# A fused linear-attention and feed-forward kernel on one core: the written order of its 1,487 steps, the engine of 188 of them and their ring places are replaced

## The chip, the cores and the metric

The kernel runs on one core of a Trainium2 chip. The metric is the device time of one execution in microseconds (us), taken as the median of several runs. A profile of one execution shows every instruction of the five engines: PE (TensorE, matrix products; its weight loads are shown as PEld), DVE (VectorE), ACT (ScalarE), POOL (GpSimd) and SP (SyncE, which issues most transfers). Times inside the profile count from its first instruction.

## The reference

Cosine-weighted linear attention over 8 batches, 8 heads, 576 tokens and 64 features per head, followed by a feed-forward layer. With `pos` the token number and `r = max(x, 0)`:

```python
def phi(x, c, s):
    r = np.maximum(x, 0.0)
    return np.concatenate([r * c, r * s], axis=-1)      # c, s = cos, sin of pi/2*pos/576
kv  = einsum('bhsf,bhsd->bhfd', phi(k), v)              # 128 x 64 per batch and head
z   = phi(k).sum(axis=2)
att = einsum('bhsf,bhfd->bhsd', phi(q), kv) / (einsum('bhsf,bhf->bhs', phi(q), z) + 1e-6)
x   = att as 4608 tokens x 512
out = leaky_relu(x @ w_in) @ w_out                      # w_in 512 x 2048, w_out 2048 x 512
```

All inputs and the output are float32 in DRAM; the kernel computes its products in float16 and sums in float32.

## The kernel before

**Tiling.** The 4,608 tokens are cut into nine groups of 512: group g below 8 holds the first 512 tokens of batch g, and group 8 the last 64 tokens of all eight batches. Each group passes the attention and then the feed-forward layer; the work of several groups overlaps.

**Attention of group g** (2 to 7 in the plain form). Loads of q, k and v (`lq`, `lk`, `lv`) go into staging slots. POOL clips q and k at zero in place (`rq`, `rk`, line 370). Eighteen half-steps `kc g.j` and `ks g.j` (j from 0 to 8; lines 376, 378 and 382, by engine ACT, POOL or DVE) multiply k by the cosine or the sine into the one tile `kp`; eight steps `q g.j.f` do the same for q. `v g.0` and `v g.1` cast v into the one tile `vm`. `kv g` is 72 small products on PE (line 440) over half of the array's rows; it needs all eighteen halves and both casts, and since `kp` and `vm` exist once, the halves of the next group cannot be written before it is through. `ko g` copies the sums out. Two transpositions by DMA, `qT g.0` and `qT g.1` (line 484), turn q; four steps `n g.j` (line 523, 8 or 16 products each) form numerator and denominator, `N g.j` divides on DVE (lines 534 to 539), and a third transposition by DMA, `xT g` (line 496), turns the result for the feed-forward layer.

**Feed-forward of group g.** Groups 0 and 1 form the first product plainly (`f`, line 603). From group 2 on both products use a seven-product scheme (Winograd's form of Strassen): sums `X g.n` of quarters of x, four units `f g.u.n` of seven products (line 742, four matmuls of 256 columns each), copies and sums of their banks (`b`, `s`, `u`, `y`, `z`, lines 388 and 656), the four activations `a`, `c`, `e`, `d` (line 766), sums `S g.n` of quarters of the activated values (line 656), products `F g.n.tt.h` (line 825, again four matmuls of 256 columns), partial sums `M g.n`, results `O g.n` and stores `D g.n`. The second product uses the scheme from group 1 on. Group 0 forms it plainly (line 626).

**Start.** `L...` load q, k, v of batches 0 and 1 and both weights; `cw` and `w` cast the weights to float16. 14 idle products, and ten more named `i.0` to `i.9` (line 307), stand on PE before there is work.

**The order.** The whole program is the string `ORDER` (line 31): every token is a step, and the loop at line 1060 emits the steps in that order. A letter behind a colon chooses the engine (`P` POOL, `A` ACT, `D` DVE); a number behind `@` chooses the ring place, that is the staging slot, output tile or PSUM place that the step's tile takes. Each engine works off its own instructions strictly in the order of the tokens; between engines semaphores hold a step until what it reads is written and what it overwrites is read. A token that stands early on one engine's list therefore says only what that engine does before and after it, not when.

```python
    engines = {"D": DVE, "A": ACT, "P": POOL}
    for token in ORDER.split():
        token, *places[:] = token.split("@")
        name, _, e = token.partition(":")
        f, args = steps.pop(name)
        f(*args, *([engines[e]] if e else []))
```

SP's list holds the loads, the stores and the 21 transpositions. A slot's next load has to wait until the last reader of the slot is through.

Of the kernel before, what the change touches and what calls it, by code (L numbers as in the profile page):

```python
# [13 lines left out]
P = 128  # L14
# [35 lines left out]
N1.0.0 F0.3.0 F0.3.2 F0.3.4 q2.3.0:P F0.3.6 kc1.6:A F0.3.8 v1.2:A lk2@0 F0.3.10 rk2 kc1.8:A  # L50
O0.2:A@1 kv1.1@0 F0.3.12 F0.3.14 ko1.1:A n1.0.1@1 N1.0.1 ks2.7:P O0.3:A@2 F0.0.14 O0.0:A@3
xt1.1.0@0 n1.1.1 N1.1.1 ks2.1:P q2.2.1:A q2.1.1:A q2.1.0:A F0.1.8 xt1.0.0@1 xt1.0.1@0 xo1.0.1:D
lv2.0@1 q2.3.1:A q2.0.0:A q2.2.0:A xo1.0.0:D kc2.2:A ks2.3:A F0.1.10 F0.1.12 xo1.1.0:D xt1.1.1@0
xo1.1.1:D kc2.3:A kc2.1:D F0.1.14 T3 kc2.6:P f1.0.0@1 f1.0.2 f1.1.0 kc2.7:A ks2.0:D f1.1.2
kc2.8:P e1.0 ks2.2:D ks2.6:A f1.10@0 f1.4.0 ks2.4:P ks2.5:A kc2.0:D f1.4.2 f1.5.0 kc2.4:D f1.5.2
# [24 lines left out]
F2.6.1.0 y3.1 kc5.0:P c3.1 n4.2 N4.2 f3.2.1 v5.0:P D2.2 f3.1.4 d3.1 lq6@3 f3.2.5 s3.2:A F2.6.1.1  # L80
q5.3.1:A n4.3 b3.2:D f3.2.6 ks5.3:P u3.2:A q5.3.0:P f3.3.1 f3.2.3 f3.2.2 kc5.2:A M2.6 N4.3 xT4
z3.2 e3.2 f3.2.7 b3.3:A y3.2 F2.5.1.1 ks5.6:A F2.7.0.0 q5.1.1:P F2.7.0.1 F2.7.1.0 F2.7.1.1
f3.3.6 ks5.2:A ks5.0:D M2.7 D1.5 a3.2 f3.3.2 f3.3.5 s3.3:D u3.3:A f3.3.7 O2.5@1 c3.2 S3.1b
f3.2.4 F2.4.0.0 q5.0.0:A d3.2 F2.4.0.1 y3.3 F2.3.0.0 lv6.0@2 ks5.4:A a3.3 F2.4.1.0 kc5.8:P
f4.0.1 F2.4.1.1 O2.4@2 f3.3.4 q5.1.0:A f3.3.3 z3.3 c3.3 X4.1:P X4.3:D F2.3.0.1 F2.3.1.0 F2.3.1.1
# [6 lines left out]
F3.5.0.0@1 D3.2 F3.7.0.0 kc6.7:P N5.2 F3.5.0.1 s4.1:A y4.1 f4.1.3 ks6.4:A rq7 z4.1 ks6.5:A d4.0
kc6.2:A ks6.2:P F3.5.1.0 kc6.4:P f4.2.5 f4.2.1 lk7@2 n5.3 F3.7.0.1 q6.3.0:A S3.4a F3.5.1.1
f4.1.4 N5.3 F3.7.1.0 F3.7.1.1 M3.7 e4.1 b4.2:A f4.2.6 s4.2:A xT5 f4.2.2 c4.1 S4.1a d4.1 S4.3a
O3.5@3 u4.2:A f4.2.3 z4.2 F3.4.0.0 F3.4.0.1 F3.4.1.0 a4.2 f4.2.7 y4.2 f4.3.1 F3.4.1.1 f4.3.5
F3.3.0.0 ks6.3:P e4.2 b4.3:A S4.2a f4.3.6 O3.4@0 D2.4 c4.2 u4.3:A S3.4b kc6.3:P X5.1:D S4.1b
f4.2.4 f4.3.2 ks6.8:A s4.3:A f4.3.7 y4.3 F3.3.0.1 F3.3.1.0 X5.2:D f4.3.3 kc6.8:P f4.3.4 kc6.1:P
# [999 lines left out]
```

## Time and profile before

| | |
|---|---|
| median of 3 runs | 276.03 us (275.15 to 276.07) |
| profiled execution: span from first to last instruction | 274.9 us |
| profiled execution: its own time | not given apart from the span; 1.1 us lie between the span and the median |
| TensorE's granted clock, mean | 0.995 |
| PE busy | 263.1 us, 96% of the span, 2,904 matmuls |
| DVE, ACT, POOL busy | 207.7, 187.5, 121.2 us |
| DMA | 57.59 MB moved, mean 209 GB/s |
| chain that ended last | PE 66%, DMA 17%, POOL 8%, DVE 4%, ACT 2% of the span |

The busy time of PE is an upper bound: the end of a matmul is modelled, and a pause shorter than the modelled tail of the matmul before it does not show. A row of a timeline gives its start, its length, the engine, the line, the operation with the tiles written and read, shapes, count, and in brackets how long the engine had been idle and what ended that.

### The profile page before, as it was taken

What the parts mean: (1) busy time and instruction counts of PE and PEld (TensorE: products, weight loads), DVE (VectorE), ACT (ScalarE), POOL (GpSimd) and SP (SyncE); (2) the same over time, 40 slices, a digit from 0 to 9 for tenths busy, and PEclk for the clock granted to TensorE, in tenths of its full rate; (3) what the DMA queues carried; (4) which work ended last, traced back from release to release, by engine and by line L of the source; (5) the groups of instructions that cost most, each with busy time, mean ns of one, the idle gap of its engine ahead of it and who ended that gap; (6) DMA issues with size and microseconds to landing.
All of it is one profiled execution on the core that took longest, in us unless ns stands there. A gap on an engine that the chain in (4) does not pass through costs nothing.

```text
span 274.9 us, 7175 instructions
## 1 busy us (share of the span) xinstructions
PE 263.1 (96%) x2904; PEld 221.6 (81%) x2904; DVE 207.7 (76%) x411; ACT 187.5 (68%) x332; POOL 121.2 (44%) x142
## 2 busy tenths in 40 slices
PE   8779999999999999999899999999999999999993
PEld 3466555555899898998799999999999899999982
DVE  4870589856989688958979978997788894588751
ACT  7845985897998879787596675675567546567300
POOL 2856223999167990975773758112114005000000
PEclk9999999999999999999999999999999999999998
DMA  7999999999999999999986693667281505020425
GB/s 235 369 393 383 399 408 374 341 198 346 185 246 295 272 205 337 290 237 281 263 297 149 102 211 113 136 129 188 70 176 55 117 17 138 1 79 0 155 55 135
DMA packets 77263, 57.59 MB, mean 209 GB/s; under 512 B 49456, under 2 KB 65840, under 8 KB 76848
## 3 DMA queue, kind: packets, MB, share of 16 engines
q1 hardware_dynamic: 76624, 56.63, 74.8%
q10 hardware_dynamic: 608, 0.52, 0.7%
q8 instruction: 22, 0.36, 0.5%
q14 instruction: 9, 0.07, 0.1%
HBM read 36.70 MB, written 9.44 MB: 168 GB/s over the span
## 4 chain that ended last, share of the span: by engine, by line
PE 66%; DMA 17%; POOL 8%; DVE 4%; ACT 2%; issue 1%; SPq 1%; POOLq 0%; DVEq 0%; ACTq 0%
PE ps L825 31%; PE ps_f L742 26%; DMA qst<-in_q_dram 5%; DMA w2st<-in_moe_w_out_dram 5%; POOL kp L378 3%; PE ps_h L603 3%; PE ps_num L523 3%; DMA w1st<-in_moe_w_in_dram 3%; DMA qpT<-qp 2%; DMA kst<-in_k_dram 2%; DVE ext L656 2%; PE ps_kv L440 2%; POOL kst L370 2%; PE ps_f L825 1%; POOL qst L370 1%
## 5 line engine op out<-in xcount | busy, mean ns | idle before, releaser
L825 PEld LDWEIGHTS <-g 128*128 128x128 f16 x640 | 62.0, 98 | 7.1 <-ACT g L612 0.2
L766 ACT ACTIVATE g<-ps_f 128x512 f16<-128x512 f32 x84 | 48.6, 597 | 22.5 <-PE ps_f L742 11.4
L825 PE MATMUL ps<-w,g 128*128 128x256 f16 x496 | 63.7, 273 | 0.0
L742 PEld LDWEIGHTS <-w 128*128 128x128 f16 x448 | 48.8, 114 | 0.9
L742 PE MATMUL ps_f<-xT,w 128*128 128x256 f16 x336 | 47.8, 273 | 0.0
L742 PEld LDWEIGHTS <-wext 128*128 128x128 f16 x336 | 36.5, 114 | 2.4 <-issue 1.6
L825 PE MATMUL ps<-T,ext 128*128 128x256 f16 x240 | 32.3, 273 | 1.1 <-DVE ext L656 1.1
L603 PE MATMUL ps_h<-xT,w 128*128 128x512 f16 (+1 forms) x144 | 29.3, 356 | 0.0
L825 PEld LDWEIGHTS <-ext 128*128 128x128 f16 x256 | 24.4, 98 | 4.0 <-DVE ext L656 1.4
L742 PE MATMUL ps_f<-X,wext 128*128 128x256 f16 x176 | 26.3, 273 | 0.9 <-ACT g L766 0.6
L656 DVE TENSOR_TENSOR ps_f<-ps_f,u 128x512 f32<-128x512 f32 x28 | 19.5, 695 | 7.3 <-PE ps_f L742 3.5
L388 ACT COPY u<-ps_f 128x512 f32<-128x512 f32 x24 | 14.1, 587 | 15.8 <-PE ps_f L742 15.8
L603 PEld LDWEIGHTS <-w 128*128 128x128 f16 x144 | 15.6, 114 | 10.1
L656 DVE TENSOR_TENSOR y<-ps_f,s 128x512 f32<-128x512 f32 x28 | 19.2, 686 | 4.5 <-PE ps_f L742 3.2
L766 ACT ACTIVATE g<-y 128x512 f16<-128x512 f32 x28 | 17.7, 632 | 4.2 <-DVE y L656 4.2
L656 DVE TENSOR_TENSOR osb<-ps,ext 128x512 f32<-128x512 f32 x23 | 15.8, 685 | 5.8 <-PE ps L825 5.0
L539 DVE TENSOR_TENSOR xs<-ps_num,rden 128x512 f16<-128x512 f32 x28 | 19.4, 692 | 1.0
L612 ACT ACTIVATE g<-ps_h 128x1024 f16<-128x1024 f32 x16 | 16.2, 1021 | 5.3 <-PE ps_h L603 5.3
L378 POOL TENSOR_SCALAR kp<-kst,cos_t 128x256 f16<-128x256 f32 x32 | 18.9, 598 | 0.2
L656 POOL TENSOR_TENSOR X<-xT,X 128x512 f16<-128x512 f16 x7 | 8.5, 1219 | 23.2 <-DVE X L656 14.3
L378 POOL TENSOR_SCALAR kp<-kst,sin_t 128x256 f16<-128x256 f32 x26 | 17.7, 683 | 1.8 <-ACT g L766 1.6
L742 PE MATMUL ps_f<-xT,wext 128*128 128x256 f16 x112 | 16.9, 273 | 0.0
(121 smaller groups left out, 478.1 us busy)
## 6 DMA issues: line engine op xcount, KB each, us to landing
out_dram<-osb SPq DMA_DIRECT2D x32, 256.0 KB, 4.1
qst<-in_q_dram SPq DMA_DIRECT2D x7, 1024.0 KB, 11.3
kst<-in_k_dram SPq DMA_DIRECT2D x6, 1152.0 KB, 7.6
vst<-in_v_dram SPq DMA_DIRECT2D x12, 576.0 KB, 6.7
w2st<-in_moe_w_out_dram SPq DMA_DIRECT2D x3, 1024.0 KB, 12.5
ext<-in_moe_w_in_dram SPq DMA_DIRECT2D x4, 512.0 KB, 9.2
vst<-in_v_dram SPq DMA_DIRECT2D x4, 288.0 KB, 6.8
kst<-in_k_dram SPq DMA_DIRECT2D x4, 288.0 KB, 6.2
```

What stands on the lines that cost most here:

```text
L370: POOL.tensor_scalar(out=t, in0=t, scalar1=FMAX, scalar2=0.0, op0=ALU.min, op1=ALU.max)
L378: eng.tensor_scalar(out=o, in0=i, scalar1=col, scalar2=1.0, op0=ALU.mult, op1=ALU.mult)
L388: nc.scalar.copy(o, i)
L440: nc.tensor.matmul(ps[:, o, (c - lo) * NE : (c - lo + 1) * NE], lhsT=st["kp", b][sl, c, j, :], rhs=vm[sl, c, j, :], start=(j == 0), stop=( ...
L523: nc.tensor.matmul(ps[lo:hi, h // 4, (h % 4) * NE : (h % 4 + 1) * NE], lhsT=qpT[:, h, lo:hi], rhs=kv[b][:, h, :],)
L539: nc.vector.tensor_tensor(out=xs, in0=ps[:, :, 0 : 4 * NE].rearrange("p a (b e) -> p a b e", e=NE)[:, :, :, 0:D], in1=rden.rearrange("p (a ...
L603: nc.tensor.matmul(ps[:, m % 2, lo:hi], lhsT=w1[m // 4, c][0][:, w1[m // 4, c][1], m % 4 : 512 : 4], rhs=xT[:, lo // P : hi // P, c, :], s ...
L612: nc.scalar.activation(g_tile(g)[:, 2 * i : 2 * i + 2, :], st["h", g, i], AF.Lrelu)
L656: eng.tensor_tensor(out=o, in0=a, in1=b, op=op)
L742: nc.tensor.matmul(ps[:, mi * HT : (mi + 1) * HT], lhsT=a[:, c, 2 * r0 + mi : 512 : 4], rhs=b[:, c], start=(n in (1, 5) and mi == 0 and c ...
L766: nc.scalar.activation(g_tile(g)[:, m : m + 2, r * HT : (r + 1) * HT], {"a": A, "c": y22, "e": E, "d": B_}[e].rearrange("p (m t) -> p m t" ...
L825: nc.tensor.matmul(ps[:, tt], lhsT=a[:, i, tt * P : (tt + 1) * P], rhs=b[:, i], start=(first and i == 0), stop=(i == NPR - 1 and (apart or ...
```

## The change

Only the string `ORDER` is replaced. The set of 1,487 steps is the same, and so are all functions. What differs is the order of the tokens, the engine letter of some steps and the ring places. In numbers of steps, before and after:

| steps | POOL | ACT | DVE |
|---|---|---|---|
| halves of k (`kc`, `ks`), groups 2 to 7 | 58, 77 | 36, 20 | 14, 11 |
| halves of q, groups 1 to 8 | 22, 32 | 30, 21 | 12, 11 |
| casts of v, groups 2 to 7 | 5, 7 | 4, 5 | 3, 0 |
| sums of x (`X`) | 11, 6 | | 17, 22 |
| sums of the first weight (`W`) | 2, 0 | | 6, 8 |
| casts of weights (`cw`, `w`) | 10, 4 | 2, 4 | 5, 9 |
| bank copies `b` | | 22, 27 | 6, 1 |

Between the same two attention steps SP's list now holds

```text
before: xT2 D0.1 lv3.1 qT3.0 qT3.1 D0.0 lk4 lv4.0 lv4.1 lq5 xT3
after:  xT2 qT3.0 lk4 D0.0 qT3.1 lq5 D0.1 lv4.0 lv4.1 xT3
```

and POOL's list, from the clipping of k of group 4 on,

```text
before: rk4 kc4.4 ks4.6 ks4.5 kc4.5 kc4.7 ks4.7 q4.1.1 v4.1 rq5 kc4.2 ks4.1 ks4.3 ks4.4 kc4.3 ks4.2 rk5
after:  rk4 kc4.4 kc4.3 ks4.3 q4.1.0 ks4.7 kc4.0 ks4.2 kc4.1 q4.1.1 q4.2.1 q4.3.1 ks4.0 ks4.8 rq5 v4.0 v4.1 q4.2.0 q4.3.0 q5.2.1 q5.3.0 q5.0.1 q5.2.0 rk5
```

The diff, cut to the lines that hold the steps spoken of:

```diff
--- before.py
+++ after.py
 ORDER = """
-Lq0.0@0 Lq0.1 q0.3.1.0:P q0.1.0.0:D Lv0.0@1 q0.1.1.0:P q0.3.0.0:D q0.0.0.1:A q0.3.0.1:A
...
-i.4@0 kv0.0@1 ko0.0:A n0.0.0@0 N0.0.0 kc0.7:A Lw1.3 cw.3:P n0.1.0 N0.1.0 kc0.0:A kv0.1@1 ko0.1:D
...
-e0.4 v1.1:D kp1.2.1 qt1.2@0 qo1.2:A F0.0.0@0 qt1.0@1 q1.1.0:D w1.2:A qo1.0:A w2.0:D w2.2:D
...
-f1.8@0 f1.9 e1.4 n2.3 N2.3 lq3@3 kc3.1:A ks3.2:A f1.14@1 f1.15 S1.1a lv3.0@0 D0.3 kc3.6:P S1.2a
...
-F1.1.0.0@1 F1.2.0.1 F1.1.0.1 lq4@1 F1.1.1.0 F1.1.1.1 M1.1:A F1.2.1.0 xT2 F1.2.1.1 F1.6.0.0@1
...
-f2.0.3 u2.0:A f2.1.1 f2.0.7 z2.0 q4.2.1:P y2.0 q4.3.1:P a2.0 f2.1.5 lk4@3 rk4 F1.5.1.0 kc4.4:P
...
-f2.3.4 X3.2:D a2.3 S2.3a F1.3.1.0 F1.3.1.1 O1.3@3 F2.1.0.0@1 d2.3 F2.1.0.1 v4.1:P kc4.1:A
...
-lk5@1 e3.0 ks4.4:P y3.0 b3.1:A kc4.3:P ks4.2:P kv4 F2.2.1.1 ko4:A rk5 ks5.5:P f3.1.6 f3.1.5
...
-q6.1.0:A kc5.6:P kv5 S3.2c S3.2a f4.1.1 v6.1:P e4.0 lk6@0 rk6 ks6.7:P f4.1.5 qT5.1 q6.2.0:P
...
-F5.2.1.0 X6.3:D F5.2.1.1 u6.0:A f6.0.7 q8.1.1:P S5.3b S5.4a kc7.8:D s6.0:A y6.0 ks7.3:A kv7
...
-F8.4.1.0 D8.5.0 O8.3.0@3 D8.3.0 D8.3.1 F8.4.1.1 O8.4@2 D8.4
...
+Lq0.0@1 Lq0.1 q0.1.0.0:P Lk0.0@0 Lk0.1 Lv0.0@3 q0.1.0.1:P q0.0.0.0:D q0.3.1.0:D q0.3.0.1:A
+q0.2.0.1:A q0.3.0.0:A q0.0.1.1:P q0.3.1.1:D v0.0:P q0.2.1.1:A q0.1.1.1:A q0.2.0.0:A q0.2.1.0:A
...
+Lw1.5 Lw1.7 Lw1.3 cw.2:P cw.1:P cw.5:P kv0.0@0 ko0.0:A qt0.2 kc0.0:D n0.0.0@0 i.1@1 qo0.2:D i.9@1
...
+f0.4.d f0.6.a@0 f0.7.a f0.6.d f0.7.d e0.3 f0.10@1 f0.11 e0.2 f0.12@0 e0.5 f0.13 F0.0.0@1 qt1.3@1
...
+f1.14@1 lv3.1 f1.15 F1.2.0.0@1 e1.4 F1.2.1.0 n2.3 kc3.3:A kc3.7:A e1.7 kc3.5:A q3.0.0:A ks3.3:A
...
+F1.7.1.0 F1.7.1.1 q3.3.0:A xT2 kc3.4:A X2.1:D f2.0.1 f2.0.5 X2.3:D W0.3:D X2.2:D kv3 b2.0:A s2.0:A
+f2.0.6 f2.0.2 f2.0.3 ko3:A W1.4:D S1.4b a2.0 qT3.0 u2.0:D q4.0.0:P X2.4:P lk4@1 rk4 kc4.4:P kc4.3:P
+ks4.3:P q4.0.1:A z2.0 f2.1.1 q4.1.0:P ks4.7:P kc4.0:P ks4.2:P f2.0.7 kc4.1:P e2.0 b2.1:A D0.0 qT3.1
+q4.1.1:P q4.2.1:P y2.0 f2.1.5 s2.1:A lq5@2 n3.0 F1.7.0.1 q4.3.1:P ks4.0:P ks4.8:P D0.1 S1.4a N3.0
+rq5 M1.7 f2.0.4 lv4.0@3 f2.1.2 f2.1.6 f2.1.3 lv4.1 d2.0 v4.0:P v4.1:P f2.2.1 n3.1 u2.1:A a2.1 c2.0
...
+F2.1.0.1 ks4.6:D ks4.4:D z2.3 kv4 lk5@1 rk5 ks5.5:P ks5.6:P kc5.1:P ks5.4:P kc5.0:P kc5.2:P kc5.4:P
+q5.3.1:P kc5.8:P ks5.1:P kc5.5:P ks5.3:P ks5.8:P ks5.2:P kc5.7:P ks5.7:P M2.1:A kc5.3:P e2.3 S2.1a
+F2.2.0.0 S2.3a X3.1:D X3.3:D X3.2:D F2.2.0.1 kc5.6:P ks5.0:P f3.0.1 b3.0:A F2.2.1.0 f3.0.5 s3.0:A
...
+y3.3 z3.3 f3.3.2 f3.3.4 xT4 c3.3 qT5.0 lk6@3 S3.1b X4.1:D F3.1.1.0 rq6 kv5 rk6 ks6.7:P a3.3 kc6.0:P
...
+f5.3.6 kv7 u5.3:A s5.3:A S4.4a O4.4@0 f5.3.7 c5.2 lq8.0@3 xT6 F5.1.0.0@1 f5.2.4 d5.2 y5.3 a5.3 S5.1b
...
+F8.7.0.0 F8.7.0.1 F8.2.0.1 F8.7.1.0 S8.4a F8.7.1.1 F8.5.1.0 O8.2:A@0 D8.2 M8.7 F8.5.1.1 F8.5.0.1
+O8.5.1@1 O8.5.0@3 S8.4b D8.5.1 F8.4.1.0 D8.5.0 F8.4.1.1 F8.4.0.0 F8.4.0.1 O8.4@2 D8.4 F8.3.1.0
+F8.3.1.1 O8.3.1@0 D8.3.1 F8.3.0.0 F8.3.0.1 O8.3.0@1 D8.3.0
```

More of the change, by code (lines that the diff above doesn't have):

```diff
@@ L50 @@
[L50 to L55, printed above, removed]
@@ L80 @@
[L80 to L85, printed above, removed]
@@ L92 @@
[L92 to L97, printed above, removed]
@@ new lines @@
+ks2.0:P ks2.4:P O0.3:A@3 n1.0.1@1 T2 lv2.1 lk3@1 N1.1.0 F0.0.12 N1.0.1 F0.0.14 n1.0.0@0 F0.1.6
+F0.1.8 n1.1.1 kc2.7:P O0.0:A@2 q2.1.0:A q2.0.0:A F0.1.10 N1.0.0 xt1.1.0@0 xt1.0.0@1 xt1.0.1@1
+F0.1.12 N1.1.1 xo1.0.1:D xo1.1.0:A q2.1.1:A F0.1.14 xt1.1.1@1 xo1.0.0:D f1.4.0 f1.0.0@0 xo1.1.1:A
+q2.3.1:A f1.0.2 f1.5.0 q2.2.0:D q2.2.1:A ks2.2:D kc2.2:A f1.5.2 f1.1.0 f1.1.2 f1.2.0@1 f1.4.2
+kc2.6:A ks2.3:D ks2.6:D e1.0 O0.1:D@1 ks2.1:A e1.2 kc2.0:A f1.2.2 f1.10@0 f1.11 rk3 kc2.1:D kc2.3:D
+kc2.8:D W0.4:D f1.3.0 f1.3.2 v2.1:A kv2 kc3.0:P T4 T3 qT2.0 lq3@3 kc3.1:P ks3.6:P rq3 q3.1.0:P e1.5
```

168 lines of the change are left out of this document (84 added, 84 removed).

## The prediction

> **What bounds the kernel now.** I read the head of the page first, then busy time by stretches, then the chain that ended last, and only then the timelines of the places that these point to. First two lines of the page, then the stretches (width, then busy time and count of PE, PEld, DVE, ACT, POOL, granted clock, share of the DMA engines, GB/s).
>
> ```profile
> span 274.9 us, 7175 instructions
> ...
> PE 263.1 (96%) x2904; PEld 221.6 (81%) x2904; DVE 207.7 (76%) x411; ACT 187.5 (68%) x332; POOL 121.2 (44%) x142
> ```
>
> ```profile
> 0.00:20.00 20.00, 15.18 (x187) 9.07 (x188) 14.12 (x39) 13.76 (x24) 11.12 (x21) 1.00 0.92 330
> 20.00:60.00 40.00, 39.82 (x388) 23.08 (x385) 25.62 (x47) 31.55 (x49) 21.15 (x19) 1.00 1.03 357
> 60.00:110.00 50.00, 49.27 (x590) 42.25 (x585) 39.77 (x85) 43.33 (x78) 32.18 (x33) 1.00 1.08 268
> 110.00:160.00 50.00, 48.66 (x595) 44.94 (x594) 42.95 (x77) 36.34 (x68) 34.35 (x41) 1.00 0.95 230
> 160.00:210.00 50.00, 50.00 (x567) 46.89 (x567) 41.12 (x85) 33.55 (x63) 17.91 (x26) 1.00 0.61 140
> 210.00:260.00 50.00, 49.96 (x505) 46.50 (x505) 38.78 (x74) 27.83 (x50) 4.47 (x5) 1.00 0.25 69
> 260.00:275.00 15.00, 10.19 (x94) 8.88 (x91) 5.38 (x10) 1.17 (x2) 0.00 (x0) 0.91 0.33 88
> ```
>
> PE sets the time from 20 us on: of its 11.8 us without work, 4.8 lie in the first 20 us, 4.8 in the last 15, and 2.3 between. But a pause shorter than the modelled tail of a matmul is not seen as idle, so I also count matmuls. Their pace comes from the chain of waits (start, length, engine, line, count):
>
> ```profile
> 157.43 0.87 PE ps L825 x8
> 158.31 1.25 PE ps_kv L440 x72
> ...
> 219.61 0.54 PE ps L825 x4
> ...
> 253.16 3.06 PE ps L825 x28
> ```
>
> A matmul of 256 columns takes 0.109 us (3.06 / 28), a step of four 0.44 (0.87 / 2), one `kv` 1.25; a step beside a change of array form takes 0.54, so a change costs about 0.10. An `n` step of eight I put at 0.26 (0.032 each, an estimate from 1.25 / 72 and 0.109). From 110 to 160 us, 595 matmuls hold two `kv` (144), six `n` (48) and 403 large ones: 2.5 + 1.6 + 43.9 = 48.0 of 50. So 2.0 us are lost there, of which 1.34 show as idle. The same count gives 1 to 2 us for 60 to 110, 1.1 for 160 to 210 and about nothing after. Past 60 us some 4 to 5 us are lost in all; 18 changes of form (five `kv` and four `n8`, in and out) take up to 1.8 of them. About 3.5 us is what a better order could win there.
>
> **What the change leaves alone.** The steps are the same, so PE has the same 2,904 matmuls. I counted the places where PE goes from the full array to half of it (`kv`, `n8`) or back: 28 in the old order and 28 in the new. At 0.10 each that is 2.8 us in both: 0. So the change can only move pauses.
>
> **The start.** 0, with bounds of -0.7 and +0.8. PE's pauses before 20 us wait for transfers and for the casts and divisions behind them:
>
> ```profile
> 12.42 0.75 PE L440 MATMUL ps_kv<-vm,kp 64*128 64x66 f16 x36
> ```
>
> ```profile
> 30.29 0.69 DVE L390 CAST w<-w2st 128x1024 f16<-128x1024 f32 x1 [1.63 <-DMA w2st<-in_moe_w_out_dram]
> ...
> 34.09 0.38 PE L626 MATMUL ps_o<-w,g 128*128 128x512 f16 x1
> ```
>
> The new order loads the same bytes in nearly the same sequence and reaches the first `kv` about as late: one 256 KB weight block now goes ahead of three parts of v, which by the 330 GB/s of the first stretch puts them some 0.8 us later, while DVE has less ahead of the first division. Whatever is won or lost is then cut off at the first product with the second weight. In the old order it stands behind 25.3 us of matmul work and ran at 34.09; the start has thus cost 8.8 us. In the new order `F0.0.0` stands behind 22.2 us (`f0.8`, `f0.9`, two transpositions and one `F0` step now follow it): 22.2 + 8.8 = 31.0. The cast of that weight ends at 30.29 + 0.69 = 30.98, and the transfer before it, unmoved in the queue, ends the wait. Three microseconds of cover are gone, and it just fits.
>
> **The inputs of `kv`.** POOL takes 19 more halves of k and ten more of q, and gives back sums and casts of weights. What this threatens is one chain: clip k when it lands, write eighteen halves, then `kv`; and the halves cannot start before the last `kv`. For group 4 the old order ran so (POOL, then SP):
>
> ```profile
> 88.51 2.11 POOL L370 TENSOR_SCALAR kst<-kst 128x2304 f32<-128x2304 f32 x1 [1.64 <-ACT u L388]
> 90.72 0.48 POOL L378 TENSOR_SCALAR kp<-kst,cos_t 128x256 f16<-128x256 f32 x1
> ...
> 93.87 0.69 POOL L378 TENSOR_SCALAR qp<-qst,sin_t 128x512 f16<-128x512 f32 x1
> 94.51 1.14 POOL L390 CAST vm<-vst 128x1152 f16<-128x1152 f32 x1
> 95.63 1.90 POOL L370 TENSOR_SCALAR qst<-qst 128x2048 f32<-128x2048 f32 x1
> ...
> 101.66 1.16 POOL L378 TENSOR_SCALAR kp<-kst,sin_t 128x256 f16<-128x256 f32 x1
> ```
>
> ```profile
> 68.48 3.41 SPq L496 DMA_TRANSPOSE xT<-xs  x1
> ...
> 73.64 6.54 SPq L484 DMA_TRANSPOSE qpT<-qp  x2
> ...
> 80.84 0.43 SPq L256 DMA_DIRECT2D kst<-in_k_dram  x1
> ```
>
> ```profile
> L378 POOL TENSOR_SCALAR kp<-kst,cos_t x32: 468/477/1425, 55.0 to 168.3; 128x256 f16<-128x256 f32 x32
> L378 POOL TENSOR_SCALAR kp<-kst,sin_t x26: 471/492/1690, 52.9 to 171.6; 128x256 f16<-128x256 f32 x26
> ...
> DMA to landing us min/median/max: 5.9/6.9/13.3
> ```
>
> ```profile
> 66.86 0.42 PE L523 MATMUL ps_num<-kv,qpT 128*128 128x66 f16 x8
> ```
>
> Now the new order, counted from the first matmul of `n2.3`. The transposition `xT2` follows 1.6 us later (66.86 to 68.48). SP then holds it for 3.4 us and the one `qT3.0` for 3.5, and issues `lk4` 6.9 after `xT2`, where the old order, with the second `qT` and two small transfers ahead, needed 12.4. So the lighter queue ahead of k is a gain of 5.5 us. Landing 6.9 (the median), clipping 2.1: 1.6 + 6.9 + 6.9 + 2.1 = 17.5. Then POOL has nine halves of k, four of q, the clipping of q5 and both casts of v: 9 x 0.48 + 4 x 0.69 + 1.90 + 2 x 1.14 = 11.3, in all 28.8. At the price that the halves had in the old stretch it is more: from 90.72 to 102.82, less 0.69, 1.14 and 1.90, twelve halves took 8.4 us, 0.70 each, and the sum is 30.8. PE comes to `kv4` after 58 steps of 0.44, five `n` and one `kv`: 27.9. It has 35.1 us for the same way in the old order. So PE waits 0.9 to 2.9 us, less up to 0.6 because the first half of `kv4` needs only the first cast of v. I take +0.5, with bounds of 0 and +2.4. I lean to the lower end because the new order puts DVE's sums with two operands in SBUF after `kv4`, and it was beside such sums that the halves took 0.70. If the cover is gone altogether, everything behind `kv4` moves by the wait. The same count for `kv5` and `kv7` leaves POOL about 2 us early at 0.48 and about 1 late at 0.70.
>
> **The small pauses past 60 us.** Two of the old ones (ACT and PE, then POOL, DVE and PE), and a sum of the same form that was not disturbed:
>
> ```profile
> 90.66 0.51 ACT L376 ACTIVATE kp<-kst,sin_t 128x256 f16<-128x256 f32 x1 [1.03 <-POOL kst L370]
> ...
> 91.71 0.60 PE L742 MATMUL ps_f<-X,wext 128*128 128x256 f16 x4 [0.56 <-ACT g L766]
> ```
>
> ```profile
> 71.37 0.75 DVE L656 TENSOR_TENSOR ext<-ext,g 128x512 f16<-128x512 f16 x2
> ...
> 132.53 2.12 POOL L370 TENSOR_SCALAR kst<-kst 128x2304 f32<-128x2304 f32 x1
> ...
> 132.67 2.25 DVE L656 TENSOR_TENSOR ext<-ext,g 128x512 f16<-128x512 f16 x1
> ...
> 134.98 0.61 PE L825 MATMUL ps<-T,ext 128*128 128x256 f16 x4 [1.13 <-DVE ext L656]
> ```
>
> At 90.66 ACT stood 1.03 us before a half of k that waited for POOL's clipping, and the activation behind it came late for PE. The new order leaves ACT 20 such halves instead of 36. At 132.67 a sum on DVE, of which two took 0.75 together at 71.37, ended only when POOL's clipping did. For the rest I counted, over both products of groups 2 to 8, how much PE work stands between a product and the product that needs its evacuation, less the evacuation itself: of 412 such links 27 have under 0.5 us to spare in the old order, 11 in the new; between `ko` and `n` the spare is 2 to 6.8 us in five of six groups, where it was 0.3 to 1.6. By that ratio, 3.5 x 16 / 27 = -2.1; since the two pauses above came from queues and not from short links, I take -1.7, with bounds of -3.5 and +0.5.
>
> The Trainium skill speaks against the change here: "SBUF — State Buffer", section "Who interferes with whom", says that VectorE and GpSimd share one pair of ports as an exclusive lock, and that a VectorE operation with two SBUF inputs fully blocks behind a GpSimd operation that reads SBUF. The rows at 132.53 and 132.67 agree: 2.25 us instead of about 0.4, ending 0.27 us after the other's end. By that rule more work on POOL means more such blocks, and this term would be positive; that is the third rival.
>
> **The end.** -0.7, with bounds of -0.9 and 0.
>
> ```profile
> 268.28 1.91 PE L825 MATMUL ps<-ext,g 128*128 128x256 f16 x16
> 268.54 0.42 DVE L656 TENSOR_TENSOR osb<-ps_f,ext 128x256 f32<-128x256 f32 x1 [0.51 <-PE ps_f L825]
> 270.23 0.69 DVE L656 TENSOR_TENSOR osb<-ps,ext 128x512 f32<-128x512 f32 x1 [1.26 <-PE ps L825]
> ```
>
> ```profile
> out_dram<-osb SPq DMA_DIRECT2D x2, 128.0 KB, 2.6
> ...
> out_dram<-osb SPq DMA_DIRECT2D x4, 64.0 KB, 2.0
> ```
>
> The old order ends with the 512-column result (0.69) and its 128 KB store (2.6); the new one with a 256-column result (0.42) and a 64 KB store (2.0): 0.27 + 0.6 = 0.9, less some queueing behind two larger stores.
>
> **The sum.** 0 + 0.5 - 1.7 - 0.7 = -1.9 on a span of 274.9: 273.0. The profiled execution's own time is not shown; its span lies 1.1 under the median of 276.03, and I carry these 1.1 over unchanged: 274.1.
>
> **The rivals.** First, **the pauses only change place**: as many queues meet as before, and 11 short links cost what 27 did. For it speaks that the two pauses quoted came from queues. Then only the end and `kv4` count: 276.0 - 0.7 + 0.2 = 275.5. That the change doesn't do what it says belongs here: the forms are as many as before, and no wait of PE in the chain is for SP.
>
> Second, slower: **POOL becomes the last input of `kv`**. Place: `kv4`, then `kv5` and `kv7`. Price: 2.4 + 1 + 1, less 0.7 at the end and 0.3 of small pauses: +3.4, 279.4. It decides from a mean of about 0.6 us per half of k on POOL. For it: 0.70 in the old stretch; POOL already 32 to 34 of 50 us busy between 60 and 160. Against: the median of 0.48.
>
> Third, **DVE held by POOL**: clippings fall on DVE's sums that PE waits for. Two more of the kind at 134.98, 2 x 1.13, with the small pauses otherwise unchanged: 276.0 + 2.3 - 0.7 = 277.6. Against: both orders have the same 16 clippings, and only one such wait of PE showed.
>
> **How the numbers follow.** Forecast 274.1: 0.48, its own range 271.8 to 275.4. First rival 0.25, second 0.17, third 0.10. What a measurement of this kernel can tell from no change is about 0.5%, 1.4 us, so faster means under 274.65. Three quarters of the forecast's chance lie there, and a quarter to a third of the first rival's: 0.36 + 0.07 = 0.43. The same: 0.12 + 0.15 + 0.01 + 0.05 = 0.33 of the four in turn. Slower: 0.24. The range for all: 271.0 to 278.5.
>
> **What would show it.** In the changed profile: 28 changes of form and the same pace of 0.109; the first second-weight product near 31; `kp` on POOL near 0.5 us in its mean, and no or under 1 us of wait before `kv4`; in the stretches from 60 to 260, less idle than 2.1 us and less than 4 us lost by count; the last store of 64 KB. A `kv` that waits for `kp` or `vm` on POOL by over 1.5 us, or DVE sums of over 2 us ahead of PE, makes me wrong, as does a first second-weight product later than 33.

## The result, and the profile after

**The new order is slower by about 0.6%.** Its median is 277.53 us (20 runs, 276.68 to 279.24) against 276.44 us for the old kernel beside it (20 runs); the ratio is 1.0060, 95% interval 1.0037 to 1.0083. This ratio, like those below, is worked out from the single runs, without those over 1.5% above the fastest of their kernel, and is not the quotient of the two medians (1.0039). The forecast was 274.1, faster. The profiled execution took 277.58 us with a span of 275.0. The first lines of its page (span; busy time of the engines):

```profile
span 275.0 us, 7178 instructions
...
PE 262.5 (95%) x2904; PEld 222.2 (81%) x2904; DVE 215.9 (79%) x411; ACT 177.3 (64%) x306; POOL 137.4 (50%) x168
```

The work has moved as the table of the change says: POOL has 16.2 us more, ACT 10.2 less, DVE 8.2 more. Where the time went shows in the stretches of the new kernel (columns as in the prediction: width, PE, PEld, DVE, ACT, POOL with counts, clock, DMA share, GB/s):

```profile
0.00:20.00 20.00, 16.23 (x193) 9.72 (x194) 13.16 (x34) 14.78 (x27) 12.68 (x23) 1.00 0.91 325
20.00:60.00 40.00, 35.43 (x298) 20.18 (x296) 28.61 (x50) 22.60 (x31) 31.94 (x26) 1.00 0.98 344
60.00:110.00 50.00, 49.72 (x630) 41.83 (x629) 45.84 (x83) 40.92 (x70) 33.02 (x39) 1.00 0.99 241
110.00:160.00 50.00, 50.00 (x624) 47.16 (x623) 42.25 (x83) 35.76 (x65) 35.77 (x50) 1.00 1.02 261
160.00:210.00 50.00, 50.00 (x588) 46.81 (x587) 42.27 (x83) 32.08 (x60) 22.88 (x31) 1.00 0.66 144
210.00:260.00 50.00, 49.98 (x482) 46.77 (x481) 37.37 (x72) 30.01 (x56) 1.16 (x1) 1.00 0.24 63
260.00:275.00 15.00, 11.17 (x103) 9.73 (x100) 6.40 (x12) 1.17 (x2) 0.00 (x0) 1.00 0.42 122
```

Only one stretch is worse, and it is the one in which the old order lost nothing: from 20 to 60 us PE is without work for 4.6 us (40 - 35.43), where it was 0.2. From 60 to 260 us it is 0.3 instead of 2.1, and the tail after the last matmul is shorter, too. Ahead of 20 us PE stands for 3.8 us instead of 4.8.

Four waits of PE make up 4.3 of these 4.6 us. PE's timeline (start, length, what it is, and in brackets the wait and what ended it):

```profile
31.39 0.59 PE L621 MATMUL ps_o<-w,g 128*128 128x512 f16 x2 [0.87 <-DVE w L385]
...
37.88 2.32 PE L621 MATMUL ps_o<-w,g 128*128 128x512 f16 x10 [0.70 <-DVE w L385]
...
45.48 0.74 PE L435 MATMUL ps_kv<-vm,kp 64*128 64x66 f16 x36 [1.32 <-POOL vm L385]
...
52.74 0.41 PE L553 MATMUL ps_numh<-kv,qpT 128*128 128x66 f16 x8 [1.43 <-DVE xs L534]
```

In order: `F0.0.0`, the first product with the second weight; `F0.3.4`, the first that needs that weight's second block; `kv1.0`, the first `kv` of group 1; and `n1.0.0`. The chain of waits of the new kernel from the landing of q of batch 1 on (start, length, what) says what lies behind the last two:

```profile
14.86 12.82 DMA qst<-in_q_dram
...
30.11 5.78 POOL qp L377 x3
...
37.27 2.93 POOL qp L377
40.20 4.61 POOL kp L377 x4
44.82 0.34 POOL vm L385
...
45.42 1.66 POOL kp L377
47.08 1.36 POOL vm L385
...
48.48 0.75 PE ps_kv L435 x36
```

POOL is never idle from 27.87 to 48.4 us: five halves of q, five of k and two casts of v, all of group 1, one behind the other, and PE's `kv1.0` waits for one of the casts. What lies behind `n1.0.0` is on DVE (its timeline, from the copy `O0.2` to the start of the division `N1.1.0`):

```profile
49.81 0.69 DVE L385 COPY osb<-ps_o 128x512 f32<-128x512 f32 x1 [1.90 <-PE ps_o L621]
50.42 1.24 DVE L651 TENSOR_TENSOR T<-w,T 128x2048 f16<-128x2048 f16 x1
51.58 0.15 DVE L529 TENSOR_SCALAR den<-ps_numh 128x8 f32<-128x8 f32 x1
```

DVE holds `O0.2` until PE has written the other bank of its tile, and behind it stand the weight sum `T2` and only then `N1.1.0`, whose result frees the place of `n1.0.0`.

Why POOL takes so long is in the groups by shape. First the old kernel up to 60 us, then the whole of the new one (busy us, mean ns of one):

```profile
L382 POOL TENSOR_SCALAR qp<-qst,cos_t 128x256 f16<-128x256 f32 x2 | 2.3, 1169 | 4.3 <-DMA qst<-in_q_dram 4.3
L378 POOL TENSOR_SCALAR qp<-qst,cos_t 128x512 f16<-128x512 f32 x1 | 0.7, 687 | 0.0
```

```profile
L373 POOL TENSOR_SCALAR kp<-kst,sin_t 128x256 f16<-128x256 f32 x41 | 23.8, 587 | 0.4
L373 POOL TENSOR_SCALAR kp<-kst,cos_t 128x256 f16<-128x256 f32 x36 | 18.3, 516 | 3.2 <-PE ps_kv L435 3.1
...
L377 POOL TENSOR_SCALAR qp<-qst,sin_t 128x512 f16<-128x512 f32 x3 | 8.0, 2683 | 0.0
L377 POOL TENSOR_SCALAR kp<-wext,cos_t 128x128 f16<-128x128 f32 x5 | 6.3, 1268 | 0.0
L377 POOL TENSOR_SCALAR qp<-qst,cos_t 128x512 f16<-128x512 f32 x2 | 4.3, 2171 | 9.5 <-DMA qst<-in_q_dram 9.5
```

There are two forms of a half on POOL. Groups 2 to 8 are clipped first (`rq`, `rk`) and then take two multiplications (line 378 before, 373 after): 0.69 us for 128x512. Batches 0 and 1 have no clipping step, so POOL takes the maximum with zero and the product in one instruction (382, 377), and that costs 1.17 us for half the size. Five halves of q of group 1, which DVE and ACT did before in 0.5 to 0.7 us each, take 12.3 us on POOL. The five halves of k of group 1, which ACT did before, and the two casts of v come on top, with 6.3 and 2.0 us.

**One count for all kernels.** PE's 2,904 matmuls at their undisturbed pace (0.109 us for 256 columns, 0.216 for 512) make about 253.8 us in every version (up to 2 us more with other prices for the small products, the same in every row), and the first starts at 1.2. What is left of a span is PE's loss up to the start of `kv2`, its loss from there to the last matmul, and the tail behind that: for the new kernel 1.2 + 253.8 + 12.8 + 3.4 + 3.8 = 275.0. Losses are from one execution each. Up to `kv2` the kernels with one and the same start agree within 0.6 us (8.5, 8.7 and 9.1 with the old one; 12.8, 12.6 and 12.8 with the new one); behind it the two profiles of the old kernel differ by 1.7.

| kernel | median us (runs) | ratio to old, 95% | loss to `kv2` | loss behind | tail |
|---|---|---|---|---|---|
| old, as shown before | 276.03 (3) | | 8.5 | 6.7 | 4.7 |
| old, second profile (`e8`) | 275.43 (1) | | 8.7 | 5.0 | 4.7 |
| new | 277.53 (20) | 1.0060 (1.0037 to 1.0083) | 12.8 | 3.4 | 3.8 |
| `e1` | 276.48 (12) | 1.0028 (1.0004 to 1.0052) | 10.6 | 4.9 | 4.0 |
| `e2` | 276.51 (12) | 1.0028 (0.9998 to 1.0058) | 12.7 | 3.9 | 3.9 |
| `e3` | 277.01 (12) | 1.0036 (1.0016 to 1.0057) | 13.5 | 3.2 | 4.0 |
| `e4` | 277.02 (12) | 1.0043 (1.0019 to 1.0066) | 11.5 | 4.2 | 3.9 |
| `e5` | **272.91** (12) | **0.9905 (0.9874 to 0.9936)** | 9.1 | 3.7 | 4.0 |
| `e6` | 278.88 (6) | 1.0120 (1.0081 to 1.0160) | 12.6 | 4.6 | 4.7 |
| `e7` | 276.61 (12) | 1.0036 (1.0006 to 1.0066) | 8.8 | 6.0 | 4.0 |
| `e9` | 276.14 (12) | 1.0019 (0.9993 to 1.0045) | 9.4 | 5.8 | 3.9 |
| `e10` | 277.19 (12) | 1.0045 (1.0022 to 1.0069) | 12.8 | 3.3 | 3.9 |

New against the old kernel's second profile: +4.1 to `kv2`, -1.6 behind, -0.8 at the end (unrounded), together +1.7, which is what the ratio makes of 276 us. The first profile was of a long execution: the median span of 35 executions of the old kernel is 273.8.

### The profile page after: what moved, and what is told of

The parts are those of the page before. It is cut to its first block, busy times and chain, and to the rows that moved or that the text cites. A ratio compares the mean times of both kernels' runs of the same rounds, so it can differ in the third digit from the quotient of the medians.

```text
span 275.0 us, 7178 instructions
## 1 busy us (share of the span) xinstructions
PE 262.5 (95%) x2904; PEld 222.2 (81%) x2904; DVE 215.9 (79%) x411; ACT 177.3 (64%) x306; POOL 137.4 (50%) x168
## 4 chain that ended last, share of the span: by engine, by line
PE 78%; DMA 7%; POOL 7%; DVE 3%; issue 2%; SPq 1%; POOLq 0%; DVEq 0%
PE ps L820 33%; PE ps_f L737 31%; PE ps_h L598 5%; DMA qst<-in_q_dram 5%; POOL kp L377 3%; POOL qp L377 3%; PE ps_kv L435 3%; PE ps_num L518 3%; DMA w1st<-in_moe_w_in_dram 3%; PE ps_f L820 1%; DVE kp L377 1%; SPq L251 1%; DVE xs L534 1%; POOL vm L385 1%; PE ps_o L621 1%
## 5 line engine op out<-in xcount | busy, mean ns | idle before, releaser
L820 PE MATMUL ps<-w,g 128*128 128x256 f16 x496 | 65.8, 273 | 0.0
L737 PE MATMUL ps_f<-xT,w 128*128 128x256 f16 x336 | 48.7, 273 | 0.0
L820 PE MATMUL ps<-T,ext 128*128 128x256 f16 x240 | 33.0, 273 | 0.0
L373 POOL TENSOR_SCALAR kp<-kst,sin_t 128x256 f16<-128x256 f32 x41 | 23.8, 587 | 0.4
L383 ACT COPY ps_f<-ps_f 128x512 f32<-128x512 f32 x27 | 15.5, 573 | 12.7 <-PE ps_f L737 12.3
L365 POOL TENSOR_SCALAR kst<-kst 128x2304 f32<-128x2304 f32 x6 | 12.9, 2158 | 17.2 <-DMA kst<-in_k_dram 10.0
L383 ACT COPY u<-ps_f 128x512 f32<-128x512 f32 x23 | 13.5, 589 | 10.8 <-PE ps_f L737 10.6
L373 POOL TENSOR_SCALAR kp<-kst,cos_t 128x256 f16<-128x256 f32 x36 | 18.3, 516 | 3.2 <-PE ps_kv L435 3.1
```

Of the source, the lines that this page charges most:

```text
L365: POOL.tensor_scalar(out=t, in0=t, scalar1=FMAX, scalar2=0.0, op0=ALU.min, op1=ALU.max)
L373: eng.tensor_scalar(out=o, in0=i, scalar1=col, scalar2=1.0, op0=ALU.mult, op1=ALU.mult)
L383: nc.scalar.copy(o, i)
L737: nc.tensor.matmul(ps[:, mi * HT : (mi + 1) * HT], lhsT=a[:, c, 2 * r0 + mi : 512 : 4], rhs=b[:, c], start=(n in (1, 5) and mi == 0 and c ...
L820: nc.tensor.matmul(ps[:, tt], lhsT=a[:, i, tt * P : (tt + 1) * P], rhs=b[:, i], start=(first and i == 0), stop=(i == NPR - 1 and (apart or ...
```

## The experiments

**Where it lies: both orders cut at `ko2`.** `e5` runs the old order up to and with `ko2` and the rest in the new one; `e6` the other way round.

```diff
-  (the order's steps up to and with ko2)
+  e5: these 307 steps in the old order, all others in the new one
+  e6: these 325 steps in the new order, all others in the old one
```

> Edit: the old order up to and with ko2 (307 steps, to about 60 us), then all other steps in the new order with the new engines; the ring places of the rest renamed at the seam so that no place is asked for before it is free. Nothing is left out. Theory (the new order loses 3.9 us more by 60 us, 12.8 against 8.9 of PE's time, and gains 2.9 behind): the 3.9 of the start come back and the gain behind stays: PE loses about 3.4 us behind 60 us; span near 271.5, time near 273.5, about 2.5 under the old kernel. Rival A (the rest looks good only because PE comes to it late and the transfers have caught up): behind 60 us PE loses 6 or more, as in the old order; time 276 to 277. Rival C (the difference lies outside the order's steps, in the time around the span): time 277.5.

> Edit: the new order up to and with ko2 (325 steps), then all other steps in the old order with the old engines; ring places of the rest renamed at the seam. Nothing is left out. Theory (losses add): the new start's 12.8 us by kv2, then 6 more behind; span near 277.7, time near 279.7. Rival A (a late PE covers the pauses behind): PE loses 3.5 to 4.5 behind kv2; time 277.0 to 278.0.

272.91 and 278.88 us: by the ratios the new rest wins 0.95% and the new start loses 1.2%, and their sum of +0.25% agrees with the +0.6% of the new kernel within the intervals. `e5` keeps the old start's 9.1 and the new rest's 3.7, and is 1% faster than the old kernel; `e6` has the new start's 12.6. Rival A, by which the rest looks good only because PE comes to it late, falls with `e5`. `e6` by itself does not decide against it: 278.88 lies between Rival A's 278.0 and the theory's 279.7, and the loss behind `kv2`, 4.6, is close to Rival A's 4.5 and under the theory's 6, which came from the long first profile; the second has 5.0. One stretch of `e5`, whose span is 271.7 us:

```profile
20.00:60.00 40.00, 39.80 (x362) 23.22 (x364) 27.47 (x50) 31.21 (x50) 20.46 (x19) 1.00 1.01 353
```

POOL has 20.5 us of work between 20 and 60 us instead of 31.9, and PE stands for 0.2.

**POOL's form.** `e1` leaves the order alone; it leaves out the clipping of the halves that POOL writes for batches 0 and 1.

```diff
-        elif eng is POOL and src in relued:
+        elif eng is POOL:
             eng.tensor_scalar(
                 out=o, in0=i, scalar1=col, scalar2=1.0, op0=ALU.mult, op1=ALU.mult
```

> Edit: the new order unchanged; on POOL every half of q and k takes the form with two multiplications (the one of 0.69 us for 128x512) instead of maximum-then-multiplication (2.1 to 2.9 us for 128x512 in the five halves of q of group 1). This leaves out the clipping at zero of those halves of batches 0 and 1 that POOL writes. Theory (the new loss between 20 and 60 us is POOL's unclipped form, in group 1): the five halves of q fall from 12.3 us together to about 3.5, the five of k from 6.3 to about 2, the cast of v that ended 0.05 us before the first kv of group 1 is through by about 43.1, and the wait of 1.3 us before that kv is gone; the wait of 1.4 us before n1.0.0 stays, since it hangs on DVE's order. Time 1.3 to 1.8 us under the new kernel, about 276.0. Rival A (the transfers of v of batch 1, now behind two weight blocks, set that kv): the halves get short but the wait stays within 0.3 us of 1.3; time unchanged, 277.5. Rival B (POOL slowed by DVE through their shared access, not by the form): the halves stay above 1.5 us; time unchanged.

POOL's timeline, then PE's `kv1.0` and the one long wait of PE that is left there:

```profile
28.09 0.96 POOL L375 TENSOR_SCALAR qp<-qst,cos_t 128x512 f16<-128x512 f32 x1 [9.40 <-DMA qst<-in_q_dram]
29.02 1.36 POOL L375 TENSOR_SCALAR qp<-qst,sin_t 128x512 f16<-128x512 f32 x2
...
36.02 3.38 POOL L375 TENSOR_SCALAR kp<-wext,cos_t 128x128 f16<-128x128 f32 x4 [3.35 <-DMA wext<-in_k_dram]
42.37 0.66 POOL L387 CAST vm<-ext 128x576 f16<-128x576 f32 x1 [2.97 <-DMA ext<-in_v_dram]
```

```profile
43.46 0.74 PE L437 MATMUL ps_kv<-vm,kp 64*128 64x66 f16 x36
...
50.51 0.41 PE L555 MATMUL ps_numh<-kv,qpT 128*128 128x66 f16 x8 [1.40 <-DVE xs L536]
```

The five halves of q fall from 12.3 to 4.6 us, those of k from 6.3 to 4.2 (2 was expected), POOL now waits for the transfers, and `kv1.0` and `F0.3.4` do not wait; `n1.0.0` does, as before. So with the transfers and DVE's list as they were, the lighter form alone frees `kv1.0`. How much of POOL's lateness came from DVE's work beside it is not shown apart: the halves of k of 128x128 still take 0.84 us each, where twice the size takes 0.48 undisturbed, and in the new kernel the unclipped ones ran from 0.71 to 1.73. The effect goes the other way too: `F0.3.4` had waited for DVE's cast of the weight, which ends at 37.18 here and at 37.83 in the new kernel, although DVE's list is the same: beside the lighter POOL the cast takes 0.78 us instead of 1.08, and the sum `W` two steps ahead of it 0.69 instead of 1.13. The loss to `kv2` falls by 2.2, but 1.5 of it come back behind, and the time falls by 1.0 instead of 1.5.

**The same halves on another engine.** `e2`:

```diff
-q1.3.0:P ... q1.2.1:P q1.1.1:P ... q1.0.0:P q1.0.1:P ... q1.3.1:D
+q1.3.1:D q1.3.0:D q1.2.1:D q1.1.1:D q1.0.0:D q1.0.1:D
```

> Edit: the new order, only the five halves of q of group 1 that POOL has go to DVE, right behind q1.3.1, into its pause of 2.2 us before the cast w0.0. Nothing is left out. Theory: POOL starts the halves of k at about 36 instead of 40.2, the last cast of v before the first kv of group 1 ends near 43.1, that kv no longer waits: 1.3 us less of PE's pauses, the wait before n1.0.0 stays; about 276.1. The cast w0.0 may end up to 0.2 us later. Rival A (transfers of v set that kv): unchanged, 277.5. Rival B (the cover of the second weight alone costs): unchanged or worse by the 0.2.

276.51, as expected to half a microsecond. `kv1.0` does not wait. The profile is of an execution 1.9 us over the median, with a granted clock of 0.96 between 20 and 60 us (1.00 in the new kernel's), so some 1.6 of its 12.7 us of loss are the clock's, an estimate from 4% of 40 us. In this execution the gain went to the next wait: DVE's `T2` now meets POOL's clipping of q and takes 2.62 us instead of 1.2, and `n1.0.0` waits 2.8. PE's `kv1.0` and `n1.0.0`, then DVE's row and POOL's:

```profile
42.88 0.74 PE L437 MATMUL ps_kv<-vm,kp 64*128 64x66 f16 x36
...
51.27 0.41 PE L555 MATMUL ps_numh<-kv,qpT 128*128 128x66 f16 x8 [2.80 <-DVE xs L536]
```

```profile
47.56 2.62 DVE L653 TENSOR_TENSOR T<-w,T 128x2048 f16<-128x2048 f16 x1
```

```profile
47.21 1.89 POOL L367 TENSOR_SCALAR qst<-qst 128x2048 f32<-128x2048 f32 x1 [2.00 <-DMA qst<-in_q_dram]
```

**The transfers of v.** `e3`:

```diff
-Lk1.1 ... Lw2.2@2 ... Lw2.3.0 Lv1.0 ... Lv1.1
+Lk1.1 Lv1.0 Lv1.1 ... Lw2.2@2 ... Lw2.3.0
```

> Edit: the new order, only the two loads of v of batch 1 go back ahead of the loads of the second weight's third and fourth blocks, right behind the load of k of batch 1. Nothing is left out. Theory (POOL is last): v lands near 37 instead of 42.4, but POOL reaches its cast at the same time; the wait before the first kv stays 1.3 within 0.3; time within 0.5 us of the new kernel, or somewhat over it since the weight blocks land 1.5 to 3 us later. Rival A (transfers set it): the wait falls to 0.3 or less, time near 276.2.

277.01, 0.5 under the new kernel. PE's timeline:

```profile
43.65 1.89 PE L623 MATMUL ps_o<-w,g 128*128 128x512 f16 x8 [0.83 <-DVE w L387]
...
46.13 0.75 PE L437 MATMUL ps_kv<-vm,kp 64*128 64x66 f16 x36 [0.15 <-POOL vm L387]
```

`kv1.0` starts at 46.13, no earlier than the 45.48 of the new kernel, and still behind POOL's cast; its wait is short only because PE comes later, held by a weight block that now lands behind v. I had expected the wait to stay 1.3, so the number missed; that `kv1.0` starts no earlier, and behind POOL's cast, shows that the transfer was not what ended the wait.

**DVE's order.** `e4`:

```diff
-n1.1.0@0 ... O0.2:D@0 ... T2 ... N1.1.0 ... T4
+n1.1.0@0 N1.1.0 ... O0.2:D@0 ... T2 T4
```

> Edit: the new order, only on DVE: the division N1.1.0 goes right behind its product, ahead of the copy O0.2 that waits for PE's last product of the other bank of its tile, and the weight sum T2 goes down to just before T4. Nothing is left out. Theory (two separate losses, POOL's and DVE's order): the first kv of group 1 waits 1.3 as before, the wait of 1.4 before n1.0.0 and the 0.3 behind F0.1.10 are gone; time 1.4 to 1.7 us under the new kernel, about 276.0. Rival A (one loss: all of it hangs on POOL's being late, and DVE's order only passes it on): the wait before n1.0.0 falls by less than 0.5; time within 0.5 of 277.5.

PE's `kv1.0` and `n1.0.0`:

```profile
46.07 0.75 PE L437 MATMUL ps_kv<-vm,kp 64*128 64x66 f16 x36 [1.33 <-POOL vm L387]
...
51.75 0.41 PE L555 MATMUL ps_numh<-kv,qpT 128*128 128x66 f16 x8
```

`kv1.0` waits 1.33, `n1.0.0` not at all: two losses, not one. The loss to `kv2` falls by 1.3, but the time only by 0.5, where 1.4 to 1.7 were expected. DVE's timeline shows where the rest went:

```profile
59.71 2.58 DVE L653 TENSOR_TENSOR wext<-w,wext 128x1024 f16<-128x1024 f16 x1
62.21 1.21 DVE L653 TENSOR_TENSOR T<-w,T 128x2048 f16<-128x2048 f16 x1
```

The first sum, 0.67 us elsewhere, ends 0.5 us after a clipping on POOL (59.61 to 61.75); then the moved `T2` stands ahead of `N2.0`.

**All three repairs.** `e7` takes `e2` and `e4` and two moves for the weight.

```diff
-... W1.1:D q1.2.0:D ... w1.0:D ... F0.0.0@1 qt1.3@1
+... w1.0:D W1.1:D q1.2.0:D ... qt1.3@1 F0.0.0@1
```

> Edit: the new order with three repairs in the start: the five halves of q of group 1 on DVE behind q1.3.1; N1.1.0 ahead of O0.2, T2 down to before T4; the cast w1.0 ahead of the sum W1.1 on DVE and the transposition qt1.3 on PE ahead of F0.0.0. Nothing is left out. Theory: the waits before kv1.0 (1.3), n1.0.0 (1.4), F0.3.4 (0.7) and half of that before F0.0.0 (0.4) are gone, 3.8 us by name; from what single repairs showed (a gain of about 1.5 by name came out as 0.4 to 1.0 in time, since kv2 and the product F1.6 then wait for halves of k and sums on DVE) some 40 to 60% of it reaches the end: time 275.2 to 276.0. Rival (all of it reaches the end): 273.7. Rival (the transfers of the start set the pace whatever the order): 277 or more.

The loss to `kv2` falls from 12.8 to 8.8. By name 3.5 of these 4 us are the waits above: `F0.0.0`, `F0.3.4` and `n1.0.0` do not wait, and `kv1.0` waits 0.84 instead of 1.32. It is still POOL's cast of v that it waits for, but POOL now casts at 42.46, when the transfer of v lands (42.41): with POOL out of the way this transfer is the next in line.

```profile
43.51 0.75 PE L437 MATMUL ps_kv<-vm,kp 64*128 64x66 f16 x36 [0.84 <-POOL vm L387]
```

But 2.6 us come back behind `kv2`'s start, and the time is 276.61, over the 275.2 to 276.0 that were expected. PE, POOL and DVE at that place:

```profile
62.45 1.10 PE L437 MATMUL ps_kv<-vm,kp 64*128 64x66 f16 x58 [2.20 <-POOL kp L375]
```

```profile
59.90 2.49 POOL L375 TENSOR_SCALAR kp<-kst,cos_t 128x256 f16<-128x256 f32 x1
```

```profile
59.61 1.39 DVE L653 TENSOR_TENSOR ext<-w,T 128x2048 f16<-128x2048 f16 x1
60.92 1.21 DVE L653 TENSOR_TENSOR w<-w 128x2048 f16<-128x2048 f16 x1
```

A half of k that takes 0.48 us undisturbed took 2.49 while DVE ran two weight sums from SBUF, and ended 0.26 us after the second: it did not get in between the two.

**The sums out of the way.** `e9`:

```diff
-N1.1.0 ... T2 T4 T3 ... N2.0
+N1.1.0 T2 ... N2.0 T4 T3
```

> Edit: the order with the three repairs, and on DVE the weight sum T2 goes up behind N1.1.0 (DVE stood 0.9 us there), T4 and T3 go down behind N2.0, which cannot run before kv2. Nothing is left out. With the three repairs PE stood 2.3 us before kv2, whose last half of k took 2.50 us on POOL (59.90 to 62.40) while DVE summed T4 and T3 from SBUF (59.61 to 62.13). Theory (POOL is held by DVE's sums from SBUF, and this is where the repairs' gain went): ks2.4 and kc2.7 take about 0.5 each, kv2 waits under 0.3, PE's loss by kv2 falls from 11.5 to 9.5 or less, time 1 to 2.3 us under the 276.6 of the three repairs: 274.3 to 275.6. Rival (the transfer of k or the clipping rk2 sets kv2): the halves may get shorter, but kv2 still waits over 1.5; time 276.6 within 0.5.

POOL's half, then DVE's moved sum with POOL's clipping beside it, then PE:

```profile
59.41 0.48 POOL L375 TENSOR_SCALAR kp<-kst,cos_t 128x256 f16<-128x256 f32 x1
...
64.34 2.44 POOL L367 TENSOR_SCALAR qst<-qst 128x2048 f32<-128x2048 f32 x1 [0.88 <-DMA qst<-in_q_dram]
```

```profile
64.94 2.91 DVE L653 TENSOR_TENSOR w<-w 128x2048 f16<-128x2048 f16 x1
```

```profile
69.03 0.42 PE L520 MATMUL ps_num<-kv,qpT 128*128 128x66 f16 x8 [1.73 <-DVE xs L536]
```

The half is at 0.48 and `kv2` does not wait, as the theory has it. The time missed its expectation all the same: 276.14, because `T3` now met POOL's clipping, `N2.1` behind it came late, and PE waited 1.73 there. Whether a better place for these sums would give the rest of the gain was not tried further; `e5`, which has all four sums done by 55 us, shows that an order without these waits exists.

**The old kernel once more, and the other way to clip.**

```diff
+  e8: the old kernel, nothing changed
+  e10: where POOL is unclipped, scalar1=col, scalar2=0.0, op0=ALU.mult, op1=ALU.max
```

> The old kernel unchanged, for a second profiled execution of it. If the pauses of the first profile belong to the order, PE again stands about 1.3 us before the unit product behind the blocked sum near 133 us and 0.7 near 91 us, and the span is 274.9 within 0.5. If they are chance meetings of POOL and DVE, which depend on how an execution runs, they lie elsewhere or are missing, and the span is near 273.8, the median span of the executions of the old kernel that ran beside the first four experiments.

> Edit: the new order unchanged; where POOL has the unclipped form it multiplies by the cosine or sine first and takes the maximum with zero second, which gives the same values since both factors are not negative. Nothing is left out. If it is the maximum in the second operation that makes POOL slow, the five halves of q of group 1 stay at 2.1 to 2.9 us and the time at 277.5. If it is the place of the constant ahead of the column, or the maximum as first operation, they fall to 0.7, as with two multiplications (0.69), and the time goes to about 276.4, as that kernel's.

`e8` has a span of 273.3. The wait of 0.65 near 92 us is there again, the 1.13 near 135 us is not: the DVE sum that had taken 2.25 there is short.

```profile
132.76 0.41 DVE L656 TENSOR_TENSOR ext<-ext,g 128x512 f16<-128x512 f16 x1
```

In `e10` the order of the two operations makes no difference to POOL (2689 and 2173 ns in the mean, 2683 and 2171 in the new kernel), and the time, 277.19, is near the new kernel's:

```profile
L379 POOL TENSOR_SCALAR qp<-qst,sin_t 128x512 f16<-128x512 f32 x3 | 8.1, 2689 | 0.0
```

## Why the prediction was wrong

**The start (0, bounds -0.7 and +0.8): this step failed; it is +4.1.** The sentence "Three microseconds of cover are gone, and it just fits" was nearly right about `F0.0.0` itself: it ran at 31.39 (forecast 31.0), and about half of its wait of 0.87 is PE's coming early. (The row at 34.09 is the second step, `F0.0.2`; the old `F0.0.0` ran at 33.21 behind 24.4 us of work, so 2.2 us of cover went and not three, and the 8.8 us stay the same.) The fault is an earlier sentence of that paragraph, that what is won or lost is "cut off at the first product with the second weight". The steps that had left the cover of `F0.0.0` now were the cover of nothing: `F0.3.4`, `kv1.0` and `n1.0.0` had lost theirs too, and I looked at none. The loss came as four waits of 0.7 to 1.4 us, so no sign that I had named showed it: `kv1.0`'s 1.32 is under the 1.5 us, and `F0.0.0` came before 33. The change's list, read through on POOL for the first 60 us and not only from group 4 on, would have shown them.

**POOL's price.** The only price for a half of q in the prediction is 0.69 us, in the sum for `kv4`; the start has no sum for POOL at all. Five of the "ten more of q" belong to group 1, which is not clipped. The row of the old kernel that prices them (1169 ns for 128x256, shown above beside a row of 0.69) doubled gives 2.3; the measured mean is 2.5, and five times the difference of 1.8 us is 9 us of POOL. The five halves of k and the two casts of v of group 1, another 8.3 us on POOL, were not counted, because the table of the change counts k and v for groups 2 to 7 only. `e2` shows that without the five halves of q `kv1.0` does not wait.

**The inputs of `kv` (+0.5, bounds 0 and +2.4): right.** The path on POOL was forecast well: from the first matmul of `n2.3` to POOL's last cast of v it took 27.7 us (forecast 28.8), and POOL was through 0.3 us before PE came to `kv4`. PE's wait of 0.28 us before the larger part of `kv4` was for a half on DVE, which ran beside POOL's casts and took 2.54 us:

```profile
102.17 1.19 PE L435 MATMUL ps_kv<-vm,kp 64*128 64x66 f16 x64 [0.28 <-DVE kp L377]
```

The clipped halves of k on POOL have means of 0.52 and 0.59 us, under the 0.6 that the second rival named. Its mechanism, POOL as the last input of a `kv`, did come, but in group 1 and not in groups 4, 5 and 7.

**The small pauses (-1.7, bounds -3.5 and +0.5): right in size.** Behind `kv2` the new order loses 3.4 us, the old one 6.7 and 5.0 in its two profiles: -3.3 and -1.6, `kv4` included. By medians the new rest, its end included, is worth 1.4 us (new kernel against `e6`) to 3.0 (`e5` against the 275.92 of the old kernel beside it). Whether the longer links or the lighter queue of ACT bring this, no run separates. One of the two old pauses on which I leaned, the blocked sum at 133 us, was a chance meeting that the second execution does not have.

**The end (-0.7): right.** The tail is 3.8 us, 0.8 to 0.9 shorter, and 3.8 to 4.0 in every kernel with the new rest, 4.7 in every one with the old.

**The time around the span.** I carried 1.1 us over; most runs of both kernels have 1.8 to 2.1. The first profile was about 1.1 longer than the old kernel's median span, so the two errors cancelled, which was luck. Put together with what was measured: +4.1 - 1.6 - 0.8 instead of 0 - 1.2 - 0.7. Had the start been 0, `e5` says what the forecast was worth: 272.91 measured, 274.1 forecast.

**The third rival**, DVE held by POOL, had a part in the start, the 0.70 us before `F0.3.4` that `e1` removes, and it is what kept the repairs from working: in the profiles of `e2`, `e4`, `e7` and `e9` time won at one place was lost where DVE's sums met POOL. The Trainium skill, "SBUF — State Buffer", section "Who interferes with whom", says that the side that comes first holds the shared ports for its whole instruction; the rows of `e7` (POOL's half 2.49 instead of 0.48 beside DVE's sums) and `e9` (DVE's sum 2.91 instead of 1.2 beside POOL) agree with it both ways. That POOL's half in `e7` stayed held over two sums in a row is what the row adds.

## What to carry to other kernels

Price each moved step by the form that it takes where it goes: the same step name on the same engine cost 0.69 or 2.5 us here, depending on whether its input had been clipped before. When a reordering takes cover away from one wait, list all consumers behind it, not the first one. And when an order loses in one stretch and wins in another, cut both orders at a common step and run both mixtures: two runs placed the difference here, and one of them, `e5`, beats both kernels, where repairing single waits moved them along.

## What the runs showed of the hardware

On POOL a product of 128x512 with a column took 0.69 us with a second multiplication behind it and 2.1 to 2.9 us with a maximum against zero before or behind it; DVE does the latter in 0.47 (undisturbed, in the new kernel at 36.35 us). The Trainium skill, "GPSIMD Engine Reference", section "4.1 Engine selection", has POOL at roughly line rate for operations with one input; for the first form the rows agree within 1.5 times DVE's 0.47, for the second they do not, and the measurement decides. Why the maximum costs so much stays open. It is not slow in every form: clipping with two constants, a minimum and a maximum, took POOL 2.11 us for 2304 columns, 0.92 ns each, where a half of 512 columns with a maximum and a column factor took over 4 ns each.

Two executions of one unchanged kernel differed by 1.6 us in span (274.9 and 273.3), and 1.1 us of that are one wait of PE where POOL's clipping met a DVE sum; a single profile is a sample of such meetings.
